# Loads in key order and a later normalisation in a fused top-k attention and Fourier-mixing kernel

## The chip, the cores and the metric

The kernel runs on one core of one Trainium2 chip. The metric is the time on the device in microseconds (us), from launch to end, as the median of several runs; less is better. A profiled execution gives, beside its time, the span from the first to the last instruction and the busy time of each engine: PE (TensorE, matrix products and transposes), DVE (VectorE), ACT (ScalarE), POOL (GpSimd), and SP (SyncE), which here does nothing but issue DMAs, in order.

## The reference

Eight batches of eight heads, 576 tokens, head size 64. Attention keeps the 32 largest scores of each row; its output, as 576 x 512 per batch, is mixed by a two-dimensional Fourier transform and goes through a normalised MLP of width 2048.

```python
def _attn_ref(q, k, v):                     # (8, 8, 576, 64)
    scores = scale * np.matmul(q, k.transpose(0, 1, 3, 2))
    kth = np.partition(scores, -32, axis=-1)[..., -32:-31]
    scores = np.where(scores >= kth, scores, -1e9)
    attn = np.exp(scores - np.max(scores, axis=-1, keepdims=True))
    attn = attn / (np.sum(attn, axis=-1, keepdims=True) + 1e-09)
    return np.matmul(attn, v)

def _moe_ref(x, w_ch1, w_ch2):              # x (8, 576, 512)
    mixed = np.real(np.fft.fft(np.fft.fft(x, axis=1), axis=2))
    u = x + mixed
    un = (u - mean(u)) / np.sqrt(var(u) + 1e-06)
    return u + np.maximum(un @ w_ch1, 0.0) @ w_ch2
```

All arithmetic is in float32.

## The kernel before

**Tiles.** Attention runs over 32 pairs of heads (four pairs to a batch, `NPB`). A pair has nine score tiles of 128 rows by 576 keys: eight for the four full blocks of 128 queries and the two heads (`e` 0 and 1), and one, with `e` None, which holds the last 64 queries of both heads (rows 0 to 63 head 0, rows 64 to 127 head 1). That makes 288 tiles, `i`, in the order of `IN_PAIR`; the shared tile is the fifth. Queries, keys and values are loaded in "halves": the 576 tokens are seen as two times 288, each as two blocks of 128 and a tail of 32, so that the five blocks of a tile are tokens 0-127, 128-255, 288-415, 416-543, and the two tails together. For the queries this is what the Fourier stage wants. Keys and values have the same order, with which any sum over keys comes out alike.

**Steps.** The program is written out by hand in a loop over steps `i` (L1468 on); the order on each engine is the order in which it is written. A step does for different tiles what they are due for: scores of tile `i + 3` on PE with their copies on ACT (`scores`, L322), the second half of the top-32 search of tile `i` and the first half of `i + 1` on DVE (`top_ops`, L388: four MAX8 and three MATCH_REPLACE8 to a tile), the bounds of tile `i` on POOL (`bounds`), mask (ACT and POOL) and exponential (ACT) of tile `i - 1`. For the pairs that `by_dma` (L419) names, 4 to 6 and 8 to 30, the probabilities are transposed by DMA: `plane(i - 2)` (L445) splits the words in two 16-bit halves on ACT and stores them in DRAM (`planes`), `turn(i - 3)` (L472) brings them back transposed into `PT`. The other pairs are transposed on PE. Head 1's rows are stored with the last 64 keys first; in the shared tile, whose rows for head 1 lie in plain order, two DMAs (L467, L468) do this turn of the keys.

**Attention's output.** A pair has two chunks of queries, 320 and 256. When the tiles of a chunk are there, `attend` (L533) multiplies them with v into a PSUM tile of tag "o", of which there is one buffer (`ps_o`, bufs=1). `attended` (L551) copies it to SBUF as `xT` (four buffers), copies the row sums to `rd` on ACT, and queues their reciprocal (L569) on DVE for the next step. In a later step `to_tokens` (L572) transposes `xT` on PE into `tpx`, again in the one buffer of "o" (from step 37 on), and `normalise` (L585) multiplies it with the reciprocals into `x`, one or two DVE instructions (L586, L593). Where DVE work is queued for the end of a step, it is in `late_now`, and what is put into `late_next` comes one step later. For batch 1 the same is done on ACT.

**When chunks go to tokens.** `attend` of a chunk is written at the end of a step, at step remainder 8 or 3 (of nine) for the pairs by DMA. Its `to_tokens` is due in the next step, but in no step that has another `attend`, and for batch b not before batch b - 2 is `written`, since `x` has two buffers. So in batches 3 to 7 some chunks wait, and then follow in neighbouring steps.

**Fourier stage and MLP.** A planner sets due steps: `at(step, where, fn)`. For batch b, whose last tile is `end`, all hangs on T0 (L1360). Batches 2 to 6 have T0 = end + 5: folds on POOL from T0 - 2 to T0 + 9, the token transform `dft_tokens` on PE (84 matmuls) at T0 + 5 and T0 + 11, the channel transform, statistics and transposes at T0 + 12 to T0 + 16. There the batch's MLP arrives in a queue of units; `level` (L1441) spreads these over the steps up to the next batch's arrival by estimates of PE time. What is left at the end of attention runs behind it.

**Loads.** `load_nat` and `load_v` (L261, L272) put six DMAs each on SP: four halves and two tails. q and k share one buffer (`nat_t`), in which k's loads follow the transposes of q (step remainder 0) and q's those of k (remainder 5); v is loaded at remainder 7, into two buffers in turn.

Of the kernel before, what the change touches and what calls it, by code (L numbers as in the profile page):

```python
# [19 lines left out]
P = 128  # L20
TH = 32
# [52 lines left out]
def kernel(  # L74
# [9 lines left out]
    nc = tc.nc  # L84
    B, H, S, D = q.shape
# [3 lines left out]
    HS = S // 2  # L89
    NC = 5  # L90
    NF = NC - 1
    TAIL = 2 * TH
# [3 lines left out]
    NPB = H // 2  # L96
    NPAIR = B * NPB
# [49 lines left out]
    nat_t = const.tile([P, NC, 2, D], F32, name="nat", tag="nat")  # L147
# [8 lines left out]
    late_now, late_next = [], []  # L156
# [69 lines left out]
    nat, qT_of, kT_of, v_of, PT, Ssb, Wk, Wp, M8, Nt = ({} for _ in range(10))  # L226
# [3 lines left out]

    def load_half(dst, src, pair, e, h, queue=None):

        b, hp = divmod(pair, NPB)
        s2 = src[b, 2 * hp + e].rearrange("(h r) d -> h r d", h=2)
        (queue or nc.sync).dma_start(
            out=dst[:, 2 * h:2 * h + 2, e, :],
            in_=s2[h, 0:2 * P, :].rearrange("(t p) d -> p t d", p=P),
        )  # L240

    def load_full(dst, src, pair):
        for e in range(2):
            for h in range(2):
                load_half(dst, src, pair, e, h)

    def load_tails(dst, src, pair, row0=(0, 0), queue=None, heads=(0, 1)):
        b, hp = divmod(pair, NPB)
        for e in heads:
            s2 = src[b, 2 * hp + e].rearrange("(h r) d -> h r d", h=2)  # L250
            for h in range(2):
                r0 = row0[e] + TH * h
                (queue or nc.sync).dma_start(
                    out=dst[r0:r0 + TH, NF, e, :], in_=s2[h, 2 * P:HS, :]
                )

    def heads_of(src, pair):
        b, hp = divmod(pair, NPB)
        return src[b, 2 * hp:2 * hp + 2].rearrange("e (h r) d -> h e r d", h=2)

    def load_nat(n, pair):  # L261
        if pair < NPAIR:
            nat[n, pair] = nat_t
            src = q if n == "q" else k
            load_full(nat_t, src, pair)
            for h in range(2):
                nc.sync.dma_start(
                    out=nat_t[TH * h:TH * (h + 1), NF, :, :],
                    in_=heads_of(src, pair)[h, :, 2 * P:HS, :].rearrange("e r d -> r e d"),
                )  # L270

    def load_v(pair):  # L272
        if pair < NPAIR:
            v_of[pair] = v_t[pair % 2]
            load_full(v_of[pair], v, pair)
            for e in range(2):
                nc.sync.dma_start(
                    out=v_of[pair][TAIL * e:TAIL * (e + 1), NF, e, :],
                    in_=heads_of(v, pair)[:, e, 2 * P:HS, :],
                )  # L280

    def prep(n, pair, blocks=((0, NF), (NF, NC))):

# [31 lines left out]
    PER_PAIR = len(IN_PAIR)  # L315
# [4 lines left out]
    N = len(items)  # L320

    def scores(i, part):  # L322

        if not 0 <= i < N:
            return 0.0
        pair, t, e = items[i]
        qT, kT = qT_of[pair], kT_of[pair]
        rows = ROWS[t]  # L330
        if part == 0:
            for n in range(1 if e is None else 2):
                Ssb[i + n] = attp.tile([P, S], F32, name=f"S_{i + n}", tag="S", bufs=6)
        q_cols = slice(P * t, P * t + rows)


        plain = (slice(0, NF * P), slice(NF * P, S))
        if e is None:
            to = [(Ssb[i], slice(TAIL * h, TAIL * (h + 1)), *plain) for h in range(2)]
        else:  # L340
            to = [
                (Ssb[i], slice(0, P), *plain),
                (Ssb[i + 1], slice(0, P), slice(TAIL, S), slice(0, TAIL)),
            ]
        if part == 1:

            copy = nc.scalar.copy if i else nc.vector.tensor_copy
            shape, name = [P, NF * P], f"sp_{i}_t"
            sp = ps_s.tile(shape, F32, name=name, tag="sp") if i else bank(shape, name)

            q_end = P * t + rows
            nc.tensor.matmul(  # L352
                sp[:, 0:P], lhsT=qT[:, q_end - P:q_end], rhs=kt_t, start=True, stop=True
            )
            for h, (s_t, r, _, tails) in enumerate(to):
                copy(out=s_t[r, tails], in_=sp[P - rows:P, TAIL * h:TAIL * (h + 1)])  # L356
            return 0.3
        if e is None and i >= PER_BATCH:

            half = NF * P // 2  # L360
            sps = [
                ps_s.tile([P, NF * P], F32, name=f"sp_{i}_{h}", tag="sp") for h in range(2)
            ]
            for g in range(2):
                for h in range(2):
                    hd = slice(D * h, D * (h + 1))
                    nc.tensor.matmul(
                        sps[h][TAIL * g:TAIL * (g + 1), 0:half],
                        lhsT=qT[hd, q_cols], rhs=kT[hd, half * g:half * (g + 1)],
                        start=True, stop=True,  # L370
                    )
            for h, (s_t, r, _, _) in enumerate(to):
                for g in range(2):
                    nc.scalar.copy(  # L374
                        out=s_t[r, half * g:half * (g + 1)],
                        in_=sps[h][TAIL * g:TAIL * (g + 1), 0:half],
                    )
            return 0.6
        for h, (s_t, r, keys, _) in enumerate(to):
            hd = slice(D * h, D * (h + 1))  # L380
            sp = ps_s.tile([P, NF * P], F32, name=f"sp_{i}_{h}", tag="sp")
            nc.tensor.matmul(  # L382
                sp[r], lhsT=qT[hd, q_cols], rhs=kT[hd, :], start=True, stop=True
            )
            nc.scalar.copy(out=s_t[r, keys], in_=sp[r])  # L385
        return 1.04
# [24 lines left out]
    def bounds(i):  # L411

        if i < N:
# [2 lines left out]
                out=Nt[i], in0=M8.pop(i)[:, 0:TOPK:TOPK - 1], in1=cc, op=ALU.mult  # L416
            )

    def by_dma(i):  # L419

        pair = i // PER_PAIR
        return NPB <= pair < NPAIR - 1 and pair != 2 * NPB - 1

    def mask(i, then=None):

# [19 lines left out]
    def plane(i, half):  # L445

        if not (0 <= i < N and by_dma(i)):
            return
        words = Wk[i].bitcast(U16).rearrange("p (h s) -> p h s", h=2)
        src = Ssb[i].bitcast(U16).rearrange("p (s h) -> p h s", h=2)  # L450
        nc.scalar.copy(out=words[:, half, :], in_=src[:, half, :])  # L451
        if half == 0:
            return
        Ssb.pop(i)
        Wk.pop(i)
        pair, t, e = items[i]
        nq = TAIL if e is None else P
        if e != 1:
            planes_of[pair, t] = dramp.tile(
                [nq, 2, 2 * S], U16, name=f"planes_{pair}_{t}", tag="planes", bufs=3  # L460
            )
        to = planes_of[pair, t]
        if e is not None:
            nc.sync.dma_start(out=to[:, :, S * e:S * (e + 1)], in_=words)
        else:
            nc.sync.dma_start(out=to[:, :, 0:S], in_=words[0:nq])
            nc.sync.dma_start(out=to[:, :, S:S + TAIL], in_=words[nq:P, :, NF * P:S])  # L467
            nc.sync.dma_start(out=to[:, :, S + TAIL:2 * S], in_=words[nq:P, :, 0:NF * P])  # L468
        if e != 1:
            Wp.pop(i)  # L470

# [100 lines left out]
    def to_tokens(pair, ch, at_once=True):  # L572

        b, hp = divmod(pair, NPB)
# [36 lines left out]
        if b == 1 and (hp, ch) != (NPB - 1, 1):  # L611
            at(now[0] + 1, "act", normalise_on_act)
        else:
            (late_now if at_once else late_next).append(normalise)
        return 0.14 * len(CHUNKS[ch])


# [289 lines left out]
    sums, summed = [], set()  # L907
# [368 lines left out]
    plan, costs, arrivals = {}, {}, []  # L1276
# [73 lines left out]
    for o, place in ((B12, w2_12), (B21, w2_21)):  # L1350
        at(PER_BATCH + 14, "load2", lambda o=o, place=place: nc.sync.dma_start(
            out=scr[:, o], in_=place
# [3 lines left out]
    for b in range(B):  # L1356
        end = PER_BATCH * (b + 1) - 1
        last = b == B - 1
        first, soon = b == 0, b == 1
        T0 = end + (2 if first else 3 if soon else 4 if last else 5)  # L1360
        if first:

            for op in fold_tails(b, nc.gpsimd):
                at(T0 - 1, "pool", op)

            def folds(b=b):
                for par, space in ((0, "own"), (1, "hT")):
                    for op in fold_ops(b, par, nc.vector, space):
                        op()
            at(T0, "dve", folds)  # L1370
            ft, fc = (T0 + 1, T0 + 1), T0 + 1
# [46 lines left out]
    queue, waiting, pending, written, now, out_next = [], [], [], set(), [0], []  # L1418
# [46 lines left out]
    for op in top_ops(0, (0, 1)):  # L1465
        op()
    i, carry = 0, 0.0
    while i < N + 5 or plan or queue or sums:  # L1468
        now[0] = i
        run(i, "begin")  # L1470
        pair_of = i // PER_PAIR
# [9 lines left out]
        e = items[j][2] if j < N else None  # L1481
# [13 lines left out]
        if pending and pending[0][0] <= i and (  # L1495
            i < 2 * PER_BATCH + 4 or chunk_at(i)[0] is None
        ):
            _, pp, pc = pending[0]
# [12 lines left out]
        if short:  # L1511
            fixed += tok
            pair, r = divmod(i - 1, PER_PAIR)
# [39 lines left out]
        pair, ch = chunk_at(i)  # L1553
# [11 lines left out]
        first, second = top_ops(i, (2, 3)), top_ops(i + 1, (0, 1))  # L1565
# [62 lines left out]
```

## Time and profile before

| | us |
|---|---|
| median of three runs | 1900.37 |
| the three runs | 1901.92, 1900.37, 1894.85 |
| profiled execution | 1894.46 |
| its span, first to last instruction | 1892.7 |
| outside the span | 1.8 |

The granted clock of PE was 0.953 on average over that execution. The DMAs that the change touches (all on SP, without the few for the very first pair; the issue is the time that SP spends on one):

| DMA | count | KB each | issue, median ns |
|---|---|---|---|
| k, halves (L237) | 124 | 64 | 461 |
| k, tails (L267) | 62 | 16 | 426 |
| v, halves (L237) | 128 | 64 | 496 |
| v, tails (L277) | 64 | 16 | 560 |
| q, halves (L237) | 128 | 64 | 468 |
| stores of the shared tile (L466, L467, L468) | 26 each | 144, 16, 128 | 581, 592, 604 |
| transposing DMA (L484) | 130 | | 2535 |

The normalisation on DVE is 57 instructions of 0.42 us (L586) and 28 of 0.27 us (L593).

How to read it: a busy share is a mean over stages with different limits. An engine's idle time counts only if the work that ends last stands behind it; where an engine waits, the profile names the instruction whose semaphore came last. A DMA is listed with its issue on SP, and SP's own waits are a view of their own.

### The profile page before, as it was taken

What the parts mean: (1) busy time and instruction counts of PE and PEld (TensorE: products, weight loads), DVE (VectorE), ACT (ScalarE), POOL (GpSimd) and SP (SyncE); (2) the same over time, 40 slices, a digit from 0 to 9 for tenths busy, and PEclk for the clock granted to TensorE, in tenths of its full rate; (3) what the DMA queues carried; (4) which work ended last, traced back from release to release, by engine and by line L of the source; (5) the groups of instructions that cost most, each with busy time, mean ns of one, the idle gap of its engine ahead of it and who ended that gap; (6) DMA issues with size and microseconds to landing.
All of it is one profiled execution on the core that took longest, in us unless ns stands there. A gap on an engine that the chain in (4) does not pass through costs nothing.

```text
span 1892.7 us, 27288 instructions
## 1 busy us (share of the span) xinstructions
PE 1720.7 (91%) x8134; PEld 1086.8 (57%) x8134; DVE 1580.9 (84%) x3301; ACT 1296.3 (68%) x3104; POOL 911.6 (48%) x1278
## 2 busy tenths in 40 slices
PE   5667699889899999999999999999999999999999
PEld 3344364365456654566456665666556655667677
DVE  7999999699899999997998998998999999862110
ACT  6878658577787777776777687767787778652100
POOL 4768643354745356354643565355544465341012
PEclk8878899899899999999999999999999999999999
DMA  5333026561567755585465854585456755430132
GB/s 166 106 93 108 20 63 167 155 158 32 137 154 191 179 132 131 135 208 141 123 157 135 228 123 124 146 218 145 124 147 172 198 129 144 122 116 6 50 101 80
DMA packets 521972, 249.19 MB, mean 132 GB/s; under 512 B 403680, under 2 KB 511841, under 8 KB 521825
## 3 DMA queue, kind: packets, MB, share of 16 engines
q1 hardware_dynamic: 521040, 247.24, 50.1%
q8 instruction: 65, 1.06, 0.2%
q14 instruction: 83, 0.67, 0.1%
q10 hardware_dynamic: 784, 0.21, 0.0%
HBM read 93.63 MB, written 84.74 MB: 94 GB/s over the span
## 4 chain that ended last, share of the span: by engine, by line
PE 64%; DVE 11%; ACT 9%; DMA 6%; POOL 5%; issue 3%; SPq 2%; POOLq 0%; DVEq 0%; ACTq 0%
PE hp L944 23%; PE cp L971 9%; PE o L542 8%; DVE m L406 5%; PE sp L382 5%; DVE wk L408 5%; PE yp L733 3%; PE cw L1141 3%; PE cv L1141 3%; PE cp L1010 3%; ACT wk L451 2%; POOL wk L430 2%; ACT wk L427 2%; DMA PT<-planes 2%; PE sp_t L352 2%
## 5 line engine op out<-in xcount | busy, mean ns | idle before, releaser
L430 POOL TENSOR_TENSOR wk<-S,wk 128x576 f32<-128x576 f32 x288 | 408.1, 1417 | 570.0 <-ACT wk L427 564.7
L406 DVE MAX8 m<-wk 128x8 f32<-128x576 f32 x864 | 626.7, 750 | 6.0
L944 PE MATMUL hp<-unT,w 128*128 128x256 f32 (+1 forms) x2048 | 533.9, 411 | 3.3 <-ACT hT L948 2.5
L944 PEld LDWEIGHTS hp<-unT,w 128*128 128x128 f32 x2048 | 378.0, 191 | 133.7 <-issue 29.9
L408 DVE MATCH_REPLACE8 wk<-m,wk 128x576 f32<-128x576 f32 x576 | 427.5, 742 | 0.0
L451 ACT COPY wk<-S 128x576 uint16<-128x576 uint16 x468 | 288.7, 666 | 0.1
L427 ACT ACTIVATE wk<-S,nt 128x576 f32<-128x576 f32 x288 | 222.3, 772 | 72.1 <-POOL nt L415 71.1
L971 PE MATMUL cp<-w,hT 128*128 128x512 f32 x512 | 247.8, 621 | 0.0
L406 DVE MAX8 m<-S 128x8 f32<-128x576 f32 x288 | 214.0, 743 | 34.5 <-ACT S L356 34.3
L542 PE MATMUL o<-PT,v 128*64 128x256 f32 (+3 forms) x1440 | 206.4, 430 | 24.9 <-DMA PT<-planes 16.7
L408 DVE MATCH_REPLACE8 wk<-m,S 128x576 f32<-128x576 f32 x288 | 213.6, 742 | 0.0
L438 ACT ACTIVATE S<-wk,nt 128x576 f32<-128x576 f32 x234 | 182.6, 781 | 43.8 <-POOL wk L430 42.6
L948 ACT ACTIVATE hT<-hp 128x320 f32<-128x320 f32 (+1 forms) x256 | 103.6, 410 | 151.5 <-PE hp L944 150.8
L382 PE MATMUL sp<-kT,qT 64*128 64x512 f32 (+1 forms) x528 | 180.3, 680 | 13.1 <-ACT means L1329 5.1
L542 PEld LDWEIGHTS o<-PT,v 128*64 128x64 f32 x1440 | 118.5, 158 | 110.5 <-issue 30.1
L971 PEld LDWEIGHTS cp<-w,hT 128*128 128x128 f32 x512 | 94.1, 197 | 110.4 <-issue 108.6
L385 ACT COPY S<-sp 128x512 f32<-128x512 f32 (+1 forms) x264 | 141.8, 587 | 18.1 <-PE sp L382 17.2
L1086 POOL TENSOR_TENSOR hT<-hT 128x512 f32<-128x512 f32 x64 | 81.4, 1275 | 99.3 <-ACT hT L948 86.4
L415 POOL TENSOR_TENSOR nt<-m,cc 128x2 f32<-128x2 f32 x288 | 58.6, 204 | 117.9 <-DVE m L406 113.9
L352 PE MATMUL sp_t<-kt,qT 128*128 128x128 f32 x320 | 71.9, 308 | 44.8 <-ACT S L374 27.4
L352 PEld LDWEIGHTS sp_t<-kt,qT 128*128 128x128 f32 x320 | 55.6, 197 | 99.2 <-ACT S L374 41.7
L1141 PE MATMUL cw<-w,hT 128*128 128x256 f32 x448 | 105.8, 383 | 0.9 <-issue 0.6
(160 smaller groups left out, 2130.4 us busy)
## 6 DMA issues: line engine op xcount, KB each, us to landing
planes<-wk SPq DMA_DIRECT2D x208, 288.0 KB
w<-w_parts SPq DMA_DIRECT2D x82, 512.0 KB
space<-in_moe_w_ch_dram SPq DMA_DIRECT2D x32, 512.0 KB
nat<-in_q_dram SPq DMA_DIRECT2D x128, 64.0 KB
v<-in_v_dram SPq DMA_DIRECT2D x128, 64.0 KB
out_dram<-x SPq DMA_DIRECT2D x32, 256.0 KB
nat<-in_k_dram SPq DMA_DIRECT2D x124, 64.0 KB
w_parts<-w_t SPq DMA_DIRECT2D x8, 512.0 KB
```

Source lines behind the costliest of these rows:

```text
L352: nc.tensor.matmul(sp[:, 0:P], lhsT=qT[:, q_end - P:q_end], rhs=kt_t, start=True, stop=True)
L382: nc.tensor.matmul(sp[r], lhsT=qT[hd, q_cols], rhs=kT[hd, :], start=True, stop=True)
L406: ops.append(lambda src=src, m8=m8: nc.vector.max(out=m8, in_=src))
L408: ops.append(lambda src=src, m8=m8: nc.vector.match_replace(w, m8, src, NEG))
L427: nc.scalar.activation(out=w, in_=Ssb[i], func=AF.Relu, scale=-FAR, bias=Nt[i][:, 1:2])
L430: nc.gpsimd.tensor_tensor(out=w, in0=Ssb[i], in1=w, op=ALU.subtract)
L438: nc.scalar.activation(out=Ssb[i] if by_dma(i) else w, in_=w, func=AF.Exp, bias=Nt.pop(i)[:, 0:1], accum_out=den_t[pair % 3][:, c:c + 1],)
L451: nc.scalar.copy(out=words[:, half, :], in_=src[:, half, :])
L542: nc.tensor.matmul(o[D * e:D * (e + 1), c0:c1], lhsT=vv[:, c, e, :], rhs=pt[:, NF if c == NF else (NF + 1) * e + c, c0:c1], start=(c == 0) ...
L944: nc.tensor.matmul(hp[:, 0:w], lhsT=w1[:, dt, P * it:P * (it + 1)], rhs=unT[:, dt, 0:w], start=(dt == 0), stop=(dt == NDT - 1),)
L971: nc.tensor.matmul(cp, lhsT=hT[:, it, P * n:P * (n + 1)], rhs=w2[:, it, :], start=(it == 0), stop=(it == NIT - 1),)
L1141: nc.tensor.matmul(dst, lhsT=h()[a][:, kc, :], rhs=rhs_of(kc), start=start and kc == 0, stop=kc == NK - 1, skip_group_check=True,)
```

## The change

Four things are changed.

1. k and v are loaded in the plain order of keys: one DMA for the 512 full keys of a head, and the last 64 keys as one block. k takes three DMAs per pair (its tail has both heads in one), v four. q keeps its halves and its six DMAs. At the start of the kernel, k's first pair still comes in halves of 256 keys, with one tail DMA per head where there were two.
2. For pairs by DMA, the score copies of the shared tile put head 1's last 64 keys first, as the tiles with `e` = 1 have them, so `plane` stores that tile with two DMAs, one per head.
3. For pairs by DMA, `normalise` goes into `late_next`: it runs at the end of the step after its transpose. Since batch 1 normalises on ACT, this concerns batches 2 to 7, without the last pair. The reciprocal keeps its place.
4. T0 of batches 2 to 6 goes from end + 5 to end + 6, and the loop's bound from N + 5 to N + 6.

```diff
     def load_half(dst, src, pair, e, h, queue=None):
-        b, hp = divmod(pair, NPB)
-        s2 = src[b, 2 * hp + e].rearrange("(h r) d -> h r d", h=2)
+        r0 = h * (HS if src is q else 2 * P)
         (queue or nc.sync).dma_start(
             out=dst[:, 2 * h:2 * h + 2, e, :],
-            in_=s2[h, 0:2 * P, :].rearrange("(t p) d -> p t d", p=P),
+            in_=head_of(src, pair, e)[r0:r0 + 2 * P].rearrange("(t p) d -> p t d", p=P),
         )
...
     def load_nat(n, pair):
         if pair < NPAIR:
             nat[n, pair] = nat_t
             src = q if n == "q" else k
-            load_full(nat_t, src, pair)
+            b, hp = divmod(pair, NPB)
+            both = src[b, 2 * hp:2 * hp + 2]
+            if n == "k":
+                for e in range(2):
+                    nc.sync.dma_start(
+                        out=nat_t[:, 0:NF, e, :],
+                        in_=both[e, 0:NF * P].rearrange("(c p) d -> p c d", p=P),
+                    )
+                nc.sync.dma_start(
+                    out=nat_t[0:TAIL, NF, :, :], in_=both[:, NF * P:S].rearrange("e r d -> r e d")
+                )
+                return
+            for e in range(2):
+                for h in range(2):
+                    load_half(nat_t, src, pair, e, h)
...
     def load_v(pair):
         if pair < NPAIR:
             v_of[pair] = v_t[pair % 2]
-            load_full(v_of[pair], v, pair)
             for e in range(2):
                 nc.sync.dma_start(
-                    out=v_of[pair][TAIL * e:TAIL * (e + 1), NF, e, :],
-                    in_=heads_of(v, pair)[:, e, 2 * P:HS, :],
+                    out=v_of[pair][:, 0:NF, e, :],
+                    in_=head_of(v, pair, e)[0:NF * P].rearrange("(c p) d -> p c d", p=P),
                 )
+            load_tails(v_of[pair], v, pair)
...
         plain = (slice(0, NF * P), slice(NF * P, S))
+        tails_first = (slice(TAIL, S), slice(0, TAIL))
         if e is None:
-            to = [(Ssb[i], slice(TAIL * h, TAIL * (h + 1)), *plain) for h in range(2)]
+            to = [
+                (Ssb[i], slice(TAIL * h, TAIL * (h + 1)), *(tails_first if h and by_dma(i) else plain))
+                for h in range(2)
+            ]
...
-            for h, (s_t, r, _, _) in enumerate(to):
+            for h, (s_t, r, keys, _) in enumerate(to):
                 for g in range(2):
                     nc.scalar.copy(
-                        out=s_t[r, half * g:half * (g + 1)],
+                        out=s_t[r, keys][:, half * g:half * (g + 1)],
...
+    def pair_by_dma(pair):
+        return NPB <= pair < NPAIR - 1 and pair != 2 * NPB - 1
...
-            nc.sync.dma_start(out=to[:, :, 0:S], in_=words[0:nq])
-            nc.sync.dma_start(out=to[:, :, S:S + TAIL], in_=words[nq:P, :, NF * P:S])
-            nc.sync.dma_start(out=to[:, :, S + TAIL:2 * S], in_=words[nq:P, :, 0:NF * P])
+            for h in range(2):
+                nc.sync.dma_start(
+                    out=to[:, :, S * h:S * (h + 1)], in_=words[nq * h:nq * (h + 1)]
+                )
...
-            (late_now if at_once else late_next).append(normalise)
+            (late_now if at_once and not pair_by_dma(pair) else late_next).append(normalise)
...
-        T0 = end + (2 if first else 3 if soon else 4 if last else 5)
+        T0 = end + (2 if first else 3 if soon else 4 if last else 6)
...
-    while i < N + 5 or plan or queue or sums:
+    while i < N + 6 or plan or queue or sums:
```

More of the change, by code (lines that the diff above doesn't have):

```diff
@@ L227, with head_of, load_tails @@
     x_of, o_of, xT_of, rd_of = ({} for _ in range(4))
+    def head_of(src, pair, e):
+        b, hp = divmod(pair, NPB)
+        return src[b, 2 * hp + e]
     def load_half(dst, src, pair, e, h, queue=None):
-        b, hp = divmod(pair, NPB)
-        s2 = src[b, 2 * hp + e].rearrange("(h r) d -> h r d", h=2)
+        r0 = h * (HS if src is q else 2 * P)
         (queue or nc.sync).dma_start(
             out=dst[:, 2 * h:2 * h + 2, e, :],
-            in_=s2[h, 0:2 * P, :].rearrange("(t p) d -> p t d", p=P),
+            in_=head_of(src, pair, e)[r0:r0 + 2 * P].rearrange("(t p) d -> p t d", p=P),
         )
[L242 to L248, printed above, removed]
-        for e in heads:
-            s2 = src[b, 2 * hp + e].rearrange("(h r) d -> h r d", h=2)
-            for h in range(2):
-                r0 = row0[e] + TH * h
+    def load_tails(dst, src, pair, queue=None, heads=(0, 1)):
+        for e in heads:
+            if src is q:
+                for h in range(2):
+                    (queue or nc.sync).dma_start(
+                        out=dst[TH * h:TH * (h + 1), NF, e, :],
+                        in_=head_of(src, pair, e)[HS * h + 2 * P:HS * (h + 1)],
+                    )
+            else:
+                r0 = TAIL * e if src is v else 0
                 (queue or nc.sync).dma_start(
-                    out=dst[r0:r0 + TH, NF, e, :], in_=s2[h, 2 * P:HS, :]
+                    out=dst[r0:r0 + TAIL, NF, e, :], in_=head_of(src, pair, e)[NF * P:S]
                 )
-    def heads_of(src, pair):
-        b, hp = divmod(pair, NPB)
-        return src[b, 2 * hp:2 * hp + 2].rearrange("e (h r) d -> h e r d", h=2)
     def load_nat(n, pair):
@@ L264, in load_nat @@
             src = q if n == "q" else k
-            load_full(nat_t, src, pair)
+            b, hp = divmod(pair, NPB)
+            both = src[b, 2 * hp:2 * hp + 2]
[12 more added lines that the diff above has]
+                    load_half(nat_t, src, pair, e, h)
             for h in range(2):
@@ L268, in load_nat @@
                     out=nat_t[TH * h:TH * (h + 1), NF, :, :],
-                    in_=heads_of(src, pair)[h, :, 2 * P:HS, :].rearrange("e r d -> r e d"),
+                    in_=both[:, HS * h + 2 * P:HS * (h + 1)].rearrange("e r d -> r e d"),
                 )
@@ L342, in scores @@
                 (Ssb[i], slice(0, P), *plain),
-                (Ssb[i + 1], slice(0, P), slice(TAIL, S), slice(0, TAIL)),
+                (Ssb[i + 1], slice(0, P), *tails_first),
             ]
@@ L417, in bounds @@
             )
+    def pair_by_dma(pair):
+        return NPB <= pair < NPAIR - 1 and pair != 2 * NPB - 1
     def by_dma(i):
-        pair = i // PER_PAIR
-        return NPB <= pair < NPAIR - 1 and pair != 2 * NPB - 1
+        return pair_by_dma(i // PER_PAIR)
     def mask(i, then=None):
@@ L465, in plane @@
         else:
-            nc.sync.dma_start(out=to[:, :, 0:S], in_=words[0:nq])
-            nc.sync.dma_start(out=to[:, :, S:S + TAIL], in_=words[nq:P, :, NF * P:S])
-            nc.sync.dma_start(out=to[:, :, S + TAIL:2 * S], in_=words[nq:P, :, 0:NF * P])
+            for h in range(2):
+                nc.sync.dma_start(
+                    out=to[:, :, S * h:S * (h + 1)], in_=words[nq * h:nq * (h + 1)]
+                )
         if e != 1:
```

## The prediction

> **What bounds the kernel now.** I read the page first (engines and slices), then the waits, busy time by stage, and last the timelines of PE, DVE and SP around the lines the change touches. The page:
>
> ```profile
> PE 1720.7 (91%) x8134; PEld 1086.8 (57%) x8134; DVE 1580.9 (84%) x3301; ACT 1296.3 (68%) x3104; POOL 911.6 (48%) x1278
> ...
> PE   5667699889899999999999999999999999999999
> ...
> DVE  7999999699899999997998998998999999862110
> ```
>
> Two engines share the work: DVE (the top-32 search) sets the pace of batch 0, PE alone the last 190 us, and between them both are near full. Stages of about one batch (columns: stretch, length, busy time and count of PE, PEld, DVE, ACT, POOL, then clock, DMA share, GB/s):
>
> ```profile
> 500.00:860.00 360.00, 330.66 (x1582) 208.27 (x1579) 337.51 (x703) 273.03 (x647) 173.19 (x252) 0.96 0.64 161
> 860.00:1070.00 210.00, 201.97 (x973) 126.90 (x970) 191.08 (x398) 159.99 (x382) 105.22 (x156) 0.98 0.60 152
> ...
> 1280.00:1490.00 210.00, 204.23 (x996) 127.39 (x992) 191.83 (x401) 162.08 (x387) 106.83 (x158) 0.98 0.63 158
> 1490.00:1700.00 210.00, 205.94 (x1012) 132.22 (x1009) 185.11 (x385) 147.69 (x355) 102.84 (x153) 1.00 0.50 132
> 1700.00:1892.00 192.00, 188.15 (x851) 140.15 (x849) 28.07 (x69) 31.21 (x78) 30.68 (x50) 1.00 0.18 59
> ```
>
> From 500 to 1700 PE is idle for 1200 - 1144.8 = 55 us. The kernel ends when PE has done all its work, so only removed PE idle (or a better clock) shortens it. What PE and DVE wait for between 500 and 1700:
>
> ```profile
> PE sp_t L352 <- ACT S L374: 23.0, 17, 3.6
> PE o L542 <- DMA PT<-planes: 7.7, 5, 3.0
> PE cp L1010 <- DMA w<-w_parts: 7.2, 2, 6.6
> ...
>   PE tpx L582: 44.9, 16
> ```
>
> The last line is the idle time before the normalisation (L586) on DVE in that stretch: 44.9 us in 16 stops. DVE arrives at the end of its step before PE has transposed the output in the same step. Those 45 us are DVE time and not span: in most of them PE is busy.
>
> **The Trainium skill.** "Perfetto Trace Analysis", Identifying the Most-Contended Engine, says to judge PE by weight-load share and not matmul busy time; here the weight loads are at 57%, so I price gains from PE's gaps and not from its 91%. "DMA: Bandwidth & Descriptors", Anatomy of one DMA, puts a semaphore wait on the issuing sequencer before dispatch; the trace agrees (SP waits 166.2 us for planes between 500 and 1700, and its later DMAs wait with it). "TensorE: Matmul & The Clock Gate", What's actually happening, says that activity releases the clock and idle time throttles it; the stages agree roughly (0.96 where PE is idle 8%, 1.00 at 2%).
>
> **Part 1, loads.** Per pair k goes from 6 DMAs to 3 (31 pairs in the loop, 93 fewer), v from 6 to 4 (64 fewer), and the shared tail's probabilities from 3 to 2 (26 fewer). In SP's timeline one pair reads (start, length):
>
> ```profile
> 1004.56 0.58 SPq L466 DMA_DIRECT2D planes<-wk  x1
> 1005.20 0.59 SPq L467 DMA_DIRECT2D planes<-wk  x1
> 1005.84 0.60 SPq L468 DMA_DIRECT2D planes<-wk  x1
> ...
> 1010.39 2.25 SPq L237 DMA_DIRECT2D v<-in_v_dram  x4
> 1012.69 1.22 SPq L277 DMA_DIRECT2D v<-in_v_dram  x2
> ...
> 1020.25 2.20 SPq L237 DMA_DIRECT2D nat<-in_k_dram  x4
> 1022.55 0.88 SPq L267 DMA_DIRECT2D nat<-in_k_dram  x2
> ```
>
> An issue costs about 0.5 us whether 16 or 288 KB follow, so per pair SP gains about 1.5 (k), 1.1 (v) and 0.65 us (planes); 93 x 0.49 + 64 x 0.52 + 26 x 0.65 = 96 us over the kernel. Bytes stay, so transfers take as long, and k and v have steps of slack. SP's free time covers nearly all of this. What shows is where the chain to an attention product runs through SP: the transposing DMA of the shared tile waits for all its stores, and attend follows one step later. PE stops there at 596.2 (2.97), 619.9 (0.80), 692.4 (0.77) and 1274.2 us (2.87), and for the weight parts behind it on SP at 854.7 (6.60); each gets up to 0.65 us. At 337.7 PE waited 7.62 us in a stretch where stores stood behind v loads: up to 1.8. Sum about 5 x 0.65 + 1 = 4 us; bounds 0 and 9. The last-key block is now filled by the copies L374 in another place; copies and sizes are the same, so nothing.
>
> **Part 2, the normalisation a step later.** One DVE step of seven search operations takes 5.1 us. In batch 6, three transposes follow one another:
>
> ```profile
> 1414.85 0.49 PE L582 MATMUL tpx<-ident,xT 128*128 128x128 f32 x3
> 1418.59 0.38 PE L582 MATMUL tpx<-ident,xT 128*128 128x128 f32 x2
> 1423.34 0.49 PE L582 MATMUL tpx<-ident,xT 128*128 128x128 f32 x3
> ...
> 1415.38 0.42 DVE L586 TENSOR_TENSOR x<-tpx,rd 128x256 f32<-128x256 f32 x1 [3.63 <-PE tpx L582]
> 1420.87 0.41 DVE L586 TENSOR_TENSOR x<-tpx,rd 128x256 f32<-128x256 f32 x1
> 1426.15 0.41 DVE L586 TENSOR_TENSOR x<-tpx,rd 128x256 f32<-128x256 f32 x1
> ```
>
> DVE was free at 1411.75 and stopped 3.63 us. After the change it searches on, is free again near 1416.9, normalises the first chunk until 1417.6, and PE asks for the single bank of tag "o" at 1418.59: no new wait, and DVE leads by 3.6 us more. The reciprocal L569, which keeps its place and needs the copies right after attend, stops some of this (about 1 of 4 us at 1284 and 1489). So DVE enters the next folding stage of batches 4 to 7 some 3 to 4 us earlier. There PE stops because ACT's mask waits for DVE's bounds and delays the score copies; the PE gaps of that kind over 0.5 us sum to about 13 us from 860 to 1600, and those of attends that came late (1064.7, 1481.2: 2.2 and 2.4, by my reading late probabilities) to 5. I take half, 9 us; bounds 0 (PE full anyway) and 25 (half of batches 2 and 3 as well).
>
> **Part 3, batches 2 to 6 mix one step later** (T0 from end + 5 to end + 6). The token transform of 4.2 us moves from the step after a pair's end into the one that computes the shared tile's scores. Its ACT copies (about 2.5 us) now stand behind the four score copies, and its matmuls between the scores and the tail product that waits for those copies. At this place PE stopped 3.56, 1.67, 1.65, 1.65 and 1.65 us (706, 921, 1130, 1339, 1545), 10.2 in all: I take 5 of it, since part 2 claims the same gaps; bounds 0 and 9. Against it: all that follows (fold, statistics, MLP, stores) shifts a step, the flush of chunks that wait for the x buffer starts a step later, and batch 6's MLP gets 24 steps where it had 25. Work is only moved, and whatever is left runs in the PE-bound end: 0, with a bound of 5 lost.
>
> **What the wait costs.** The "o" bank is held a step longer. Behind a transpose that waits for it stand all of PE's later work, then ACT's copies, and only two steps on DVE. Holding PE's and DVE's times as they are and setting each normalisation one step on, the next claim comes too early (batch 6: 1418.59, where the next step's normalisation ends at 1420.87 + 0.9, so 3.2) by 7.2 us in batch 3 (755.40 against 762.6), 8.0 in batch 4 (three places), 8.4 in 5, 6.6 in 6 and 5.3 in 7: 35.6 us. In batches 4 to 7 DVE had stood waiting there, so its own step comes earlier by as much and the stall goes, as worked out above. In batch 3 DVE is the late one (transpose done 752.0, normalised 754.68, no wait), so a stall stays: once, since afterwards PE is the one behind. I take 4 us of the 7.2, as a 2.39 us wait at 759 falls into it; bounds 0 and 12.
>
> **Sum.** -4 - 9 - 5 + 4 = -14; the three gains share gaps, so I take -13. The profiled execution took 1894.46 us (span 1892.7 and 1.8 around it), so 1881.5. The median of the three runs is 5.9 us above it; on that scale 1887.
>
> **Rivals.**
> - No change that shows: PE is full anyway, and the gaps removed come back as other gaps (1895 to 1905 on the median's scale). For it: PE is at 96 to 98% from 860 on. Against it: the gaps are of one kind and follow DVE.
> - Slower: the "o" bank becomes the coupling. If the score tiles or the reciprocal keep DVE from running ahead, all 35.6 us of claims turn into PE stalls, less about 10 of parts 1 and 3: 1926. It decides as soon as, at the second of two transposes in neighbouring steps, DVE's next step ends after PE's claim, in more than about half of the eleven places. For it: eleven places are too early as they stand, and reciprocals wait 7.1 us in one place. Against it: at the first of nearly every group DVE was waiting for PE.
> - A larger gain: PE was held by DVE more than its gaps show, and the clock, 0.96 to 0.98, rises too. Most of the 45 us come back: 1860.
>
> **Numbers.** Forecast 0.52, no change 0.23, slower 0.18, larger gain 0.07. The forecast's own range is 1872 to 1894; the range to hold eight in ten goes from 1866 into the slower case, 1911. What a measurement can tell from no change is about 0.5%, or 9.5 us: of the forecast 0.44 lies beyond it, 0.07 within and 0.01 on the other side. Faster 0.51, same 0.30, slower 0.19.
>
> **What would show it.** Right: the stops of L586 on tpx between 500 and 1700 fall from 44.9 to under 12 us, SP issues 183 fewer DMAs in the loop, PE's idle from 500 to 1700 falls from 55 to about 43, and the waits of L352 on L374 fall from 23 by a third. Wrong: new waits of L582 or L542 on x L586 or L593 above 10 us, or DVE's stops moving to L569 or to the score tiles with PE's idle unchanged.

## The result, and the profile after

The change makes the kernel slower: 1915.22 us (median of five runs, 1913.04 to 1916.54) against 1894.85 us for the kernel before on the same chip (1889.88 to 1901.92), a ratio of 1.009 with a 95% interval of 1.0065 to 1.0115, or some 17 us. (The five runs of the kernel before are the three given above and two more. The two medians lie 20 us apart; all differences in us from here on are taken from the ratio.) The profiled execution has a span of 1913.5 us where the one before had 1892.7. The time lies outside the range that was given, and on the other side of the forecast.

Engines and slices of the page, the changed kernel:

```profile
PE 1728.1 (90%) x8134; PEld 1092.8 (57%) x8134; DVE 1586.1 (83%) x3301; ACT 1296.8 (68%) x3104; POOL 909.9 (48%) x1278
...
PE   6566698889898998989999898989999999999999
...
DVE  8999999799999999988899897989999899862110
```

The same 8134 PE instructions are busy 7.4 us longer, and PE idles more. Its stages (stretch, length, busy time and count of PE, PEld, DVE, ACT, POOL, clock, DMA share, GB/s):

```profile
500.00:860.00 360.00, 329.47 (x1564) 208.75 (x1558) 340.74 (x710) 278.21 (x659) 173.30 (x251) 0.96 0.63 161
860.00:1070.00 210.00, 199.50 (x949) 124.00 (x950) 187.54 (x390) 153.17 (x365) 102.22 (x152) 0.98 0.59 148
1070.00:1280.00 210.00, 195.19 (x906) 119.34 (x904) 183.73 (x381) 151.99 (x362) 98.83 (x149) 0.95 0.54 137
1280.00:1490.00 210.00, 200.48 (x964) 126.58 (x964) 192.69 (x400) 157.90 (x375) 105.02 (x156) 0.98 0.61 156
1490.00:1700.00 210.00, 205.21 (x1004) 133.21 (x1005) 187.47 (x389) 149.56 (x356) 104.58 (x156) 0.98 0.58 148
```

Line numbers are those of each kernel: L561, L601 and L390 here are L542, L582 and L374 in the kernel before. `sp` and `sp_t` are scores, of the full keys and of the last 64; `us` is ACT's copy of the channel transform, `tpu` the transposes behind it, and `cp` and `cw` are products of the MLP.

From 500 to 1700 us PE is idle 1200 - 1129.9 = 70.1 us, 15 more than before, most of it from 1070 to 1490. The waits of PE in that stretch show what came and what went (waiter, what released it, us in total, times, longest):

```profile
PE tpu L878 <- ACT us L830: 11.5, 4, 2.9
PE cp L1029 <- DMA w<-w_parts: 10.0, 4, 5.1
PE o L561 <- DMA PT<-planes: 8.8, 3, 3.9
PE cw L1160 <- DMA w<-w_parts: 7.8, 2, 4.5
PE sp L398 <- ACT kT L318: 7.8, 3, 4.0
PE tpx L601 <- DVE x L612: 5.9, 4, 4.8
PE sp_t L368 <- ACT S L390: 4.3, 8, 1.7
PE o L561 <- DVE x L612: 2.5, 1, 2.5
```

The waits of DVE there, in the same columns:

```profile
DVE m L422 <- ACT S L372: 58.4, 52, 6.9
DVE rd L588 <- ACT rd L587: 28.5, 14, 5.3
```

The two waits that the change was expected to remove are gone: DVE does not stop for tpx at all (44.9 us before), and the score product of the last 64 keys waits 4.3 us for the score copies (23.0 before). In their place PE has four waits that were small or absent: for weight parts (17.8 us; 7.2 before), for the copies of the channel transform (11.5; 1.4), for k's transposed copy (7.8; none of note) and for the normalisation (5.9; 0.6; a product of attend waits another 2.5 us for it). DVE's stops have moved to the score tiles (58.4 us; 23.9 before) and the reciprocal (28.5; 13.5).

### The profile page after: what moved, and what is told of

Same layout as the page of the kernel before. It is cut to its first block, busy times and chain, and to the rows that moved or that the text cites. A ratio compares the mean times of both kernels' runs of the same rounds, so it can differ in the third digit from the quotient of the medians.

```text
span 1913.5 us, 26918 instructions
## 1 busy us (share of the span) xinstructions
PE 1728.1 (90%) x8134; PEld 1092.8 (57%) x8134; DVE 1586.1 (83%) x3301; ACT 1296.8 (68%) x3104; POOL 909.9 (48%) x1278
## 4 chain that ended last, share of the span: by engine, by line
PE 63%; DVE 13%; ACT 9%; POOL 5%; DMA 5%; issue 3%; SPq 2%; POOLq 0%; DVEq 0%; ACTq 0%
PE hp L963 21%; PE cp L990 9%; PE o L561 7%; DVE m L422 5%; PE sp L398 5%; DVE wk L424 5%; PE cw L1160 4%; PE cv L1160 4%; PE cp L1029 3%; PE yp L752 3%; ACT wk L445 2%; DMA w<-w_parts 2%; POOL wk L448 2%; PE sp_t L368 2%; ACT wk L469 1%
## 5 line engine op out<-in xcount | busy, mean ns | idle before, releaser
L561 PE MATMUL o<-PT,v 128*64 128x256 f32 (+3 forms) x1440 | 200.5, 424 | 24.3 <-DMA PT<-planes 16.6
L561 PEld LDWEIGHTS o<-PT,v 128*64 128x64 f32 x1440 | 116.3, 156 | 106.1 <-issue 32.5
L1160 PEld LDWEIGHTS cw<-w,hT 128*128 128x128 f32 x448 | 84.4, 195 | 29.0 <-issue 12.6
L398 PEld LDWEIGHTS sp<-kT,qT 64*128 64x128 f32 (+1 forms) x528 | 48.1, 194 | 83.6 <-issue 30.2
```

The costliest lines, as they stand in the source:

```text
L398: nc.tensor.matmul(sp[r], lhsT=qT[hd, q_cols], rhs=kT[hd, :], start=True, stop=True)
L561: nc.tensor.matmul(o[D * e:D * (e + 1), c0:c1], lhsT=vv[:, c, e, :], rhs=pt[:, NF if c == NF else (NF + 1) * e + c, c0:c1], start=(c == 0) ...
L1160: nc.tensor.matmul(dst, lhsT=h()[a][:, kc, :], rhs=rhs_of(kc), start=start and kc == 0, stop=kc == NK - 1, skip_group_check=True,)
```

## The experiments

Every ratio is against the kernel before, timed on the same chip. Three sets of runs follow: each part by itself, then the later T0 taken to pieces, then the reloads of weights.

### Each part by itself

`loads` has only the loads and the two stores of the shared tile; the loop's bound goes back with T0:

```diff
-            (late_now if at_once and not pair_by_dma(pair) else late_next).append(normalise)
+            (late_now if at_once else late_next).append(normalise)
...
-        T0 = end + (2 if first else 3 if soon else 4 if last else 6)
+        T0 = end + (2 if first else 3 if soon else 4 if last else 5)
```

> Only parts 1 and 2 of the change: k and v in key order, the shared tile stored with two DMAs; the normalisation and T0 as before. Theory 'step' (the later T0 is what costs): 0 to 5 us faster than before, with about 183 fewer DMAs on SP. Theory 'bank' (the single buffer of o, held longer, costs): the same, 0 to 5 us faster. Theory 'loads' (the new order of DMAs delays others): 10 to 20 us slower.

Measured: 0.9962 (0.9949 to 0.9975), 7.2 us faster, a little more than the 0 to 5 expected. SP issues 184 DMAs fewer, and the sum of its issue times falls by 74 us (858.7 to 784.4) rather than the 96 estimated: the larger DMAs take a little longer to issue (k full 0.55 us where a half took 0.46, k tail 0.67 for 0.43). PE's idle time over the span falls by 4.6 us (172.0 to 167.4). The waits of attend for PT between 500 and 1700 fall from 7.7 to 5.7 us, but other waits of attend take their place: all of them together are 13.0 us before and 12.6 here. The wait of 7.62 us at 337.7 is still there, with 7.7. So the gain is shown, but not that it comes by way of attend. Theory "loads" falls.

`late_norm` has only the later normalisation. The last chunk of a batch keeps its place, since with T0 at end + 5 the fold reads it in the next step:

```diff
-            (late_now if at_once else late_next).append(normalise)
+            ends_batch = (hp, ch) == (NPB - 1, 1)
+            late = pair_by_dma(pair) and not ends_batch
+            (late_now if at_once and not late else late_next).append(normalise)
```

> Only the later normalisation, with T0 at end + 5; the last chunk of each batch, which the fold needs one step later, is normalised at once as before. Theory 'step': -8 to +4 us, and DVE's stops for tpx between 500 and 1700 fall from 45 to under 15 us. Theory 'bank': 10 to 20 us slower, with waits of tpx and o on x. Theory 'loads': 0.

Measured: 1.004 (1.0023 to 1.0057), 7.6 us slower, between what theory "step" (up to 4) and theory "bank" (10 to 20) expected. DVE's stops for tpx fall to 2.4 us as expected, and still it costs. PE's timeline in batch 3 (start, length, what, idle time before it):

```profile
750.55 0.49 PE L586 MATMUL tpx<-ident,xT 128*128 128x128 f32 x3
...
753.16 0.66 PE L367 MATMUL sp<-kT,qT 64*64 64x256 f32 x8
760.97 0.66 PE L586 MATMUL tpx<-ident,xT 128*128 128x128 f32 x2 [7.15 <-DVE x L597]
```

The second of two neighbouring transposes waits 7.15 us for the bank. There DVE was late already. In batches 4 to 7 one such wait comes, of 2.1 us in batch 6. DVE's stops, first in the kernel before and then in this one:

```profile
DVE x L586 <- PE tpx L582: 44.9, 16, 5.9
DVE m L406 <- ACT S L356: 23.9, 12, 3.3
DVE rd L569 <- ACT rd L568: 13.5, 4, 7.1
```

```profile
DVE m L406 <- ACT S L356: 58.1, 43, 5.2
DVE rd L573 <- ACT rd L572: 24.2, 7, 9.7
...
DVE x L590 <- PE tpx L586: 2.4, 4, 0.7
```

58.1 + 24.2 + 2.4 = 84.7 us; before, the same three were 23.9 + 13.5 + 44.9 = 82.3. The sum has not come down: where DVE no longer stops for the transposes, it stops for the score copies and the row sums that ACT delivers.

`late_mix` has only T0 at end + 6.

> Only T0 of batches 2 to 6 at end + 6. Theory 'step': 15 to 25 us slower, with the waits of PE for weight parts behind the seven products of batches 3 to 6 (together some 15 us) and of tpu for the copies of the channel transform (2.9 us each in batches 4 to 7). Theory 'bank': 0 to 5 us faster. Theory 'loads': 0.

Measured: 1.0118 (1.0097 to 1.0138), 22.4 us slower, within the 15 to 25 that theory "step" expected. This is the part that costs. `loads_late_norm` is the change without it (with the last chunk of a batch normalised at once, as in late_norm):

> The whole change without the later T0 (T0 at end + 5; the last chunk of each batch is normalised at once). Theory 'step': 3 to 12 us faster than before, the best of the four. Theory 'bank': 10 to 20 us slower. Theory 'loads': 10 to 20 us slower.

Measured: 0.9983 (0.9966 to 1.0000), 3.2 us faster: the gain of the loads, less some of what the later normalisation costs. It is not the best of the four, as theory "step" expected; `loads` is. Theory "bank" as the main cost falls. The three parts alone sum to -7.2 + 7.6 + 22.4 = 22.8 us, where the whole change measures 17; so they are not quite independent. (The whole change also normalises the last chunk of a batch a step later, which late_norm leaves out.)

`late_norm_4to7` leaves batch 3 (and 2) out of the later normalisation, to see what DVE's lead is worth where no stall comes with it:

```diff
-            late = pair_by_dma(pair) and not ends_batch
+            late = b >= 4 and pair_by_dma(pair) and not ends_batch
```

> The later normalisation in batches 4 to 7 alone (not in 2 and 3, not the last chunk of a batch). If the cost of late_norm is the one stall of tpx in batch 3 (7.1 us) and DVE's lead is worth the 9 us of the prediction: 6 to 10 us faster than before. If the lead is worth nothing: within 3 us of before, with no wait of tpx on x above 1 us.

Measured: 1.002 (1.0009 to 1.0031), 3.8 us slower; neither expectation holds in full, and nothing is gained. The stall of batch 3 is gone. The cost is 3.8 us where it was 7.6, but the two intervals overlap. Of what is left, attend's waits from 500 to 1700 grow from 13.0 to about 17.8 us (why was not tried), and in batch 6, at the very place for which the prediction worked out "no new wait", the second transpose stops for 2.06 us:

```profile
1417.53 0.49 PE L586 MATMUL tpx<-ident,xT 128*128 128x128 f32 x3
...
1419.01 2.42 PE L950 MATMUL hp<-unT,w 128*128 128x320 f32 x8
1423.49 0.41 PE L586 MATMUL tpx<-ident,xT 128*128 128x128 f32 x2 [2.06 <-DVE x L597]
...
1412.58 0.17 DVE L573 RECIPROCAL rd<-rd 128x4 f32<-128x4 f32 x1
...
1422.74 0.41 DVE L590 TENSOR_TENSOR x<-tpx,rd 128x256 f32<-128x256 f32 x1
1423.08 0.27 DVE L597 TENSOR_TENSOR x<-tpx,rd 64x128 f32<-64x128 f32 x1
```

The same reciprocal in the kernel before:

```profile
1406.59 0.17 DVE L569 RECIPROCAL rd<-rd 128x4 f32<-128x4 f32 x1
```

DVE does not stop here any more, but it comes to the place with less of a lead over PE than before: its reciprocal stands 5.0 us ahead of the first transpose (1412.58 and 1417.53), where in the kernel before it stood 8.3 us ahead (1406.59 and 1414.85). Its three kinds of stops sum to 47.5 + 20.9 + 13.0 = 81.4 us from 500 to 1700, so it has gained nothing on the way.

### The later T0 taken to pieces

`mix_two_later` sets T0 to end + 7, to tell a cost of each step's delay from a cost of where the steps fall.

> T0 of batches 2 to 6 at end + 7. Theory 'places': not twice the cost of late_mix, but anything between 0 and 30 us slower than before, by other waits. Rival 'delay' (each step by which the MLP comes later costs by itself): 40 to 50 us slower.

Measured: 1.0104 (1.0084 to 1.0124), 20 us slower and not 45. The delay by itself isn't it; the places are.

`bounds_first` is late_mix with one exchange on POOL, in one step of each of batches 2 to 6:

```diff
+        ahead = i in [PER_BATCH * (b + 1) + 13 for b in range(2, B - 1)]
+        if ahead:
+            bounds(i)
         run(i, "pool0")
         some_sums(max(2.1 - planned, 0.0))
-        bounds(i)
+        if not ahead:
+            bounds(i)
```

What it is about is seen in late_mix's timelines. POOL's:

```profile
944.04 1.27 POOL L1000 TENSOR_TENSOR x<-x,hT 128x512 f32<-128x512 f32 x1 [2.81 <-ACT hT L998]
945.26 0.19 POOL L632 COPY fg<-zw 128x4 f32<-128x4 f32 x1
945.41 1.40 POOL L629 TENSOR_TENSOR fg<-zw 128x254 f32<-128x254 f32 x2
946.77 1.69 POOL L629 TENSOR_TENSOR fg<-fg 128x128 f32<-128x128 f32 x4
...
948.58 0.19 POOL L415 TENSOR_TENSOR nt<-m,cc 128x2 f32<-128x2 f32 x1
```

ACT's, from the mask on:

```profile
948.80 0.78 ACT L427 ACTIVATE wk<-S,nt 128x576 f32<-128x576 f32 x1 [4.84 <-POOL nt L415]
...
950.83 0.59 ACT L306 COPY kT<-tpk 128x512 f32<-128x512 f32 x1
```

PE's:

```profile
951.47 1.13 PE L382 MATMUL sp<-kT,qT 64*128 64x512 f32 x4 [2.31 <-ACT kT L306]
```

DVE's:

```profile
950.92 0.76 DVE L406 MAX8 m<-S 128x8 f32<-128x576 f32 x1 [5.20 <-ACT S L356]
```

POOL runs the MLP's addition and the fold's third operation and only then the bounds; ACT's mask waits for those; behind the mask in ACT's order stand the score copies and k's copy; and so PE and DVE wait as well. The exchange puts the bounds ahead of the fold's 3.3 us (945.26 to 948.58) and leaves the addition where it is. Before the change this fold step stood one step earlier, ahead of a step that transposes no keys.

> late_mix, with POOL's bounds put ahead of the fold's third operation in the one step where that operation now stands before the step that transposes k. Theory 'places': 5 to 9 us faster than late_mix (13 to 17 slower than before); PE's waits for kT (7.8 us) and DVE's two longest waits for scores in batches 4 and 5 go. Rival 'fold': back to within 5 us of before.

Measured: 1.0066 (1.0047 to 1.0085), that is 9.9 us faster than late_mix, just above the 5 to 9 expected; PE's waits for kT are gone from its list, and DVE's waits for scores fall from 29.2 to 16.7 us.

`channels_late` moves only what follows the token transform:

```diff
-            ft, fc = (T0 + 5, T0 + 11), T0 + 12
+            ft, fc = (T0 + 5, T0 + 11), T0 + 13
```

> T0 as before; only the channel transform, the statistics and the MLP's arrival of batches 2 to 6 come one step later, folds and token transforms stay. Theory 'places' (the later T0 costs by what its steps collide with, most of it in the channel transform and the MLP): 10 to 18 us slower than before, with tpu waiting for us (about 10 us) and cp and cw for weight parts (over 10 us). Rival 'fold' (the fold's longest step before the bounds is what costs): 0 to 4 us slower.

Measured: 1.017 (1.0147 to 1.0193), 32 us slower, nearly twice the upper end of what was expected. tpu waits 11.4 us for us, and cp 21.8 us for weight parts, so these two come with the later channel transform and MLP; but the sum was not foreseen.

### The reloads of weights

The MLP of a chunk multiplies by quarters of w2, with seven products where eight would be usual. It reloads quarters of w2 from DRAM between its products (`bring`, L884, on SP), and each reload waits until PE has read the old content. In late_mix, at the end of batch 4. SP's timeline:

```profile
1077.52 2.78 SPq L484 DMA_TRANSPOSE PT<-planes  x1
1080.40 0.60 SPq L464 DMA_DIRECT2D planes<-wk  x1
1081.09 1.16 SPq L887 DMA_DIRECT2D w<-w_parts  x2
```

PE's over the same steps:

```profile
1070.80 2.91 PE L542 MATMUL o<-PT,v 128*64 128x320 f32 x20 [1.62 <-DMA PT<-planes]
...
1073.96 1.89 PE L1141 MATMUL cw<-w,hT 128*128 128x256 f32 x8
...
1076.24 1.89 PE L1141 MATMUL cw<-w,hT 128*128 128x256 f32 x8
...
1078.39 1.07 PE L1010 MATMUL cp<-w,hT 128*64 128x512 f32 x2
1086.35 3.68 PE L1010 MATMUL cp<-w,hT 128*64 128x512 f32 x6 [6.89 <-DMA w<-w_parts]
```

The last of the seven products now stands behind the attention product of the pair's end, and the MLP's product for the tail of the tokens (`cp`), which needs the reloaded weights, follows at once. The reload is issued only at 1081.09, behind a transposing DMA of 2.78 us and a store on SP, and PE waits 6.89 us for it. In the kernel before, a reload went out at 1062.57, right behind `cw`, and it is the attention product that stands between the two (PE's timeline of that kernel):

```profile
1060.54 1.99 PE L1141 MATMUL cw<-w,hT 128*128 128x256 f32 x8
1064.72 2.91 PE L542 MATMUL o<-PT,v 128*64 128x320 f32 x20 [2.19 <-DVE x L1099]
...
1067.98 1.94 PE L1010 MATMUL cp<-w,hT 128*64 128x512 f32 x8
```

In late_mix such waits sum to 21.1 us from 500 to 1700, 13.9 more than before:

```profile
PE cp L1010 <- DMA w<-w_parts: 14.3, 4, 6.9
...
PE cw L1141 <- DMA w<-w_parts: 6.8, 2, 3.5
```

Three kernels leave these reloads out, all 82 of them, and one more leaves them out of bounds_first. Their products use other weights; the instructions of the engines are the same:

```diff
-        nc.sync.dma_start(out=dst, in_=scr[:, o, kcs, :])
+        if isinstance(place, list):
+            nc.sync.dma_start(out=dst, in_=scr[:, o, kcs, :])
```

> The kernel before without the reloads of parts of w2 between the seven products (they are left out in every batch, so the products use other weights). 5 to 15 us faster than before: PE's waits for weight parts (7.2 us from 500 to 1700, and more of PE's weight loads) go, and SP has 82 DMAs fewer.

> late_mix without the same reloads (left out in every batch). Theory 'places': of the 22 us between late_mix and before, 10 to 15 are waits for weight parts and what hangs on them, so 7 to 12 us slower than before_no_reload. Rival (weight waits only stand in for other waits): still about 20 us slower than before_no_reload.

> channels_late without the same reloads (left out in every batch). Theory 'places': of the 32 us between channels_late and before, 15 to 20 go, so 12 to 17 us slower than before_no_reload. Rival: still about 30 us slower than before_no_reload.

> late_mix with both taken away: the bounds ahead of the fold's third operation, and no reloads of parts of w2 (left out in every batch). If the two together are what the later T0 costs: within 4 us of before_no_reload (1861 to 1869). If something else of the later T0 costs as well (the transposes that wait for the channel transform's copies, 11.5 us), 6 to 12 us slower than before_no_reload.

| | with reloads | without |
|---|---|---|
| before | 1 | 0.9831 (0.9808 to 0.9854) |
| late_mix | 1.0118 (1.0097 to 1.0138) | 0.9886 (0.9868 to 0.9904) |
| bounds_first | 1.0066 (1.0047 to 1.0085) | 0.9832 (0.9808 to 0.9855) |
| channels_late | 1.0170 (1.0147 to 1.0193) | 1.0066 (1.0044 to 1.0088) |

Read down the second column: without reloads the later T0 costs 0.0055, or 10 us, and with the bounds put first nothing at all. Read across: with the bounds first, the later T0 costs 12.5 us with reloads and none without. So its 22 us are the reloads (some 12) and the fold ahead of the bounds (some 10), and on balance nothing of size is left. The waits for the copies of the channel transform add nothing on balance: bounds_first_no_reload has their 11.5 us in full and is level with before_no_reload. Against them stands what the later T0 was meant to win, the waits for the score copies (24.1 us there, 7.0 here). That the 12 us come from collisions like the one above agrees with the 13.9 us of waits for weight parts; but leaving the reloads out takes away everything that they do on SP and on the DMA engines, so the collision by itself is not shown apart.

Two expectations failed. Reloads cost the kernel before itself 32 us, not 5 to 15. And channels_late does not lose its excess without them (it grows from 32 to 45 us, the latter against before_no_reload): scores then wait for ACT's copies of the scores of the last 64 keys (L356) (19.3 us in 7 places). That kernel is no part of the change, and its own cost stays open.

### A version that beats both

`loads_bounds_first` is `loads` with the same exchange on POOL, in the step where the fold's third operation stands with T0 at end + 5.

> The kernel loads (parts 1 and 2, T0 and normalisation as before), with POOL's bounds put ahead of the fold's third operation in its one step per batch (2 to 6). If that operation holds ACT's mask up there as in late_mix: 2 to 6 us faster than loads, so 9 to 13 us faster than before, and DVE's waits for scores of 3.3 us in batches 3 to 7 go. If PE sets the pace there anyway: within 1.5 us of loads.

Measured: 0.9949 (0.9933 to 0.9966), 1888.86 us. It is the fastest of the kernels that leave nothing out, but its interval overlaps that of `loads`, and DVE's waits for scores are as they were (22.5 us; 23.6 in loads). So the loads by themselves are shown to beat both kernels; that the exchange helps at this place is not shown.

## Why the prediction was wrong

- **The bound.** Right in the main. The time follows PE's idle time from 500 to 1700 us in the profiled executions: 53.0 us in loads (0.9962), 55.2 before (1), 60.7 in late_norm_4to7 (1.002), 64.2 in late_norm (1.004), 64.3 in bounds_first (1.0066), 70.2 in the changed kernel (1.009), 71.9 in late_mix (1.0118), 83.1 in channels_late (1.017). Two stand out of this order: loads_late_norm with 60.8 us at 0.9983 and mix_two_later with 74.4 us at 1.0104.
- **Part 1, loads: -4, bounds 0 and 9.** Right in sign and within its bounds: -7.2 us. The way is not confirmed: attend's waits from 500 to 1700 fell by 0.4 us in all, and the wait at 337.7, for which up to 1.8 us were counted, did not shrink.
- **Part 2, the later normalisation: -9.** Wrong. The stops for the transposes went, but not "DVE leads by 3.6 us more" nor "so DVE enters the next folding stage ... earlier": in batch 6 of late_norm_4to7 DVE's lead is 3.3 us smaller than before, and over 1200 us the sum of its stops is 82.3 us before, 84.7 in late_norm and 81.4 in late_norm_4to7. The stops went to the score tiles and the reciprocal, as the prediction's last sentence names as a sign of failure. Even without the stall of batch 3 the part costs 3.8 us.
- **What the wait costs: +4.** The mechanism was right, and so was the place of the long stall, batch 3. The frozen timeline gave 7.2 us and 4 was taken; late_norm measured 7.15 there, the changed kernel 4.8 and another 2.5 at the next product of attend. That batches 4 to 7 have no stall was wrong in one place, batch 6: 2.1 us in late_norm and late_norm_4to7, 0.6 in the changed kernel.
- **Part 3, T0: -5.** This is the step that decided. The gap that it was to close did close (waits on L374 from 23.0 to 4.3 us, more than foreseen). What failed is the sentence "Work is only moved, and whatever is left runs in the PE-bound end: 0, with a bound of 5 lost": the move cost 22 us, by two collisions that could have been looked for. The prediction followed the token transform into its new step, and not the fold's operations on POOL and the MLP's last product with its reloads on SP. It did not follow the channel transform either, whose copies brought 10 us of new waits (1.4 to 11.5) against the 18.7 that were won.
- **The sum.** Forecast -13, measured +17. Of these 30 us, part 3 has 27 (22 where -5 stood), the later normalisation with its wait 13 (8 where -5 stood), and the loads take 3 off; the parts taken alone overshoot the 30 by some 7.
- **The rivals.** The one on the slow side had the right sign by the wrong mechanism: it gave the "o" bank 35.6 us, where the runs give the later normalisation 7.6 in all. That the change came out slower, as this rival said, is no support for it.

## What to carry to other kernels

Where a schedule is written by step, moving a block by one step can cost by its neighbours and not by the delay: one step cost 22 us here, two steps 20. List every instruction that the block issues on every engine and DMA queue, and for each look at what then stands behind it in that queue's order; here these were a fold of 3.3 us ahead of a 0.2 us instruction that three engines wait for (some 10 us in five batches), and reloads of weights whose cover was taken away (some 12). And a stop of an engine is not won when it goes, if the engine stops a step later for something else: 42 us of stops went, and their sum stayed.

## What the runs showed that was not expected

- The waits that name a DMA underprice it. PE's waits for weight parts from 500 to 1700 were 7.2 us, and leaving the reloads out made the kernel 32 us faster. PE's idle time there fell by 16 us (55.2 to 39.0). Beside the 7.2, nearly all of this is attend's, whose waits fell from 13.0 to about 4 us:

```profile
PE o L542 <- DMA PT<-planes: 2.3, 2, 1.8
...
PE o L542 <- DVE m L406: 1.7, 2, 1.1
```

  So the reloads held up the transposed probabilities too; whether on SP or on the DMA engines was not tried. Busy time over the execution, for the same 8134 instructions, fell by another 13.6 us (1720.7 to 1707.1), 7.4 of it in the attention products (206.4 to 199.0).
- What an idle microsecond on PE costs beside itself is not shown. From before to late_mix, idle time from 500 to 1700 rose by 16.7 us and busy time over the execution by 7.1 (1720.7 to 1727.8; clock 0.953 to 0.944). The Trainium skill ("TensorE: Matmul & The Clock Gate", What's actually happening) says that the default state is throttled and that activity releases it, and this pair agrees in direction. Other pairs do not: the changed kernel is busy 7.4 us longer at the same clock of 0.953, and late_norm, with 9.0 us more idle time, is busy 3.7 us less (1717.0; clock 0.952).
- A DMA's issue on SP depends a little on its shape: k's tail of both heads in one DMA took 0.67 us, one of its former halves 0.43.
